# Gated linear attention followed by a GELU feed-forward: query scaling on GpSimd, with other group sizes and another load order

## The chip, the cores and the metric

The kernel runs on one core of one Trainium2 chip. The metric is the device time of one execution in microseconds; the kernel before has a median of 206.8 us in three runs (206.2 to 206.98). The profiled execution spans 205.2 us. A core has five engines that run their own instruction streams and meet at semaphores: TensorE (PE, with its weight loads as PEld), VectorE (DVE), ScalarE (ACT), GpSimd (POOL) and SyncE (SP, which here only issues DMAs).

## What is computed

For each of 4 batches and 8 heads, with 768 time steps and head dimension 48, a 48x48 state is decayed by a sigmoid gate, updated with an outer product and read by the query. The result, as 3072 tokens of 384 numbers, goes through a feed-forward with exact GELU.

```python
f = 1 / (1 + exp(-f_logit))                        # [4, 8, 768, 48]
for t in range(768):
    state = f[:, :, t, :, None] * state + einsum('bhd,bhe->bhde', k[:, :, t], v[:, :, t])
    y[:, :, t] = einsum('bhd,bhde->bhe', q[:, :, t], state)
x = y.transpose(0, 2, 1, 3).reshape(3072, 384)
out = gelu(x @ w_in) @ w_out                       # w_in 384x2048, w_out 2048x384
```

## The kernel before

The 3072 tokens are 24 chunks of 128, six per batch. Inside a chunk the recurrence is written with the running sum G of log f: keys are multiplied by exp(-G), queries by exp(G), and a masked 128x128 product per head takes the place of the loop. Across chunks a state is carried.

The Python program builds a list of operations, each with an engine, an assumed duration, its inputs and the buffers that it uses. A list scheduler (`Plan`) places them at assumed times, and the instructions are then emitted in the order of those times, so that each engine's stream is a fixed order worked out beforehand. An operation with `alt` may be placed on a second engine, if that lets it start earlier.

```python
for eng, dur in ((o.eng, o.dur),) if not o.alt else ((o.eng, o.dur), o.alt):
    ...                                    # t: when buffers, inputs and this engine are free
    cand.append((t, o, eng, dur))
for t, o, eng, dur in cand:
    ...
    key = (int((t + (self.bias if o.alt and eng == "ACT" else 0)) * 20 + 0.999), o.prio, o.seq, t + dur)
```

So the earliest start in steps of 0.05 us is taken, then the lowest priority number. The plan counts an input load as 1.05 us and gives weight DMAs a length on the DMA engines; it has no time on GpSimd for issuing one.

The settings, the weight load and the steps of a chunk n that matter here:

```python
SIZES = [4, 2, 2, 4, 4, 4, 4]              # chunks per feed-forward group
ORDER = ['c0', 'c1', 'c2', 'c3', 'O3', 'W0', 'W1', 'O1', 'c4', 'O0', 'O2']   # load order, then c5, c6, ...
EARLY = 1.5                                # weight DMAs are emitted this much ahead of their planned time
RMAJOR = 0; KBALT = 1; ALTN = 6; BIAS = 0.8; SEED = 0
BATCH = [1, 1, 1, 1, 1, 1, 2, 2, 2, 2, 2, 4, 2, 1, 1]    # chunks per exp/ln batch of the gate

def load_win(kk, half, ch):                # W0, W1: halves of the 2048 columns, 6 DMAs each
    p0, p1, r0 = ((0, 96, 96 * kk), (96, 128, 288 + 32 * kk))[half]
    cs = slice(ch * d_ff // 2, (ch + 1) * d_ff // 2)
    return nc.gpsimd.dma_start(out=win[p0:p1, kk, cs], in_=moe_w_in[r0:r0 + p1 - p0, cs])

# [...] chunk_in: f_logit, k, q, v of a chunk by four DMAs from SP
# [...] stage1: ACT exp, ACT ln -> lf; PE sums it into gps; ACT exp(G) -> gt, ACT exp(-G) -> rg
P.add("DVE", 0.57, ... nc.vector.tensor_tensor(kp, kt, rg, ALU.mult), name=f"KP{n}")     # L359
P.add("DVE", 0.57, ... nc.vector.tensor_tensor(qp, qt, gt, ALU.mult), name=f"QP{n}")     # L363
P.add("POOL", 0.52, ... nc.gpsimd.tensor_copy(vp, vt), name=f"VC{n}")                    # L369
# [...] attn: PE transposes kp and qp (L406); DVE copies kb, in two halves, for n < 6 on ACT if
#       earlier; ACT copies qT, for n < 6 on DVE if earlier; PE multiplies them (L425);
#       DVE masks the product into am (L429)
# state: PE S (L441), DVE R: rr = S + old (L456), POOL T: tn = rr * gl (L458), POOL SB: sb = bf16(tn), twice (L464)
# y: PE multiplies vp by am and sb by qT into yp (L477, L481)
# x: yp goes to xT by one copy (96x384) and three small ones (32x128), DVE, for n < 6 on ACT if earlier
# ffn_group: F1, PE: 3 matmuls win by xT per 512 columns of hps (L515); ACT gelu to gT (L519);
#            F2, PE: 16 matmuls gT by wout per chunk (L532); copy osb (L219 or L221); store by SP (L540)
```

A later pass makes the first load of a chunk wait for an earlier weight DMA, where weights were planned within 3 us before it: it takes the last weight DMA that was planned over 2.5 us before the load. Before the chain of work begins to fill the PE, short matmuls on a constant (`trin`, L587) are put into its gaps in the first 26 us.

Of the kernel before, what the change touches and what calls it, by code (L numbers as in the profile page):

```python
# [55 lines left out]
SWITCH = 1.28  # L56
JITTER = 2.0


class Op:  # L60
    __slots__ = ("eng", "dur", "fn", "bufs", "prio", "deps", "table", "start", "end", "vis", "seq", "name", "alt", "nb")


class Plan:


    def __init__(self, seed=0, bias=0.0):
        self.ops, self.w, self.r = [], {}, {}
        self.rnd, self.bias = random.Random(seed) if seed else None, bias

    def add(self, eng, dur, fn, rd=(), wr=(), bufs=(), prio=0.0, deps=(), table=None, name="", alt=None):
        o = Op()
        o.alt, o.nb = alt, 0.0
        o.eng, o.dur, o.fn, o.bufs, o.prio, o.table, o.name = eng, dur, fn, tuple(bufs), prio, table, name
        o.start = o.end = o.vis = None
        o.seq = len(self.ops)
        d = list(deps)
        for k in rd:
            d += self.w.get(k, [])
        for k in wr:  # L80
            d += self.w.get(k, []) + self.r.get(k, [])
        for k in rd:
            self.r.setdefault(k, []).append(o)
        for k in wr:
            self.w[k] = [o]
            self.r[k] = []
        o.deps = list({id(x): x for x in d if x is not o}.values())
        for b in o.bufs:
            b.users.append(o)
        self.ops.append(o)  # L90
        return o
# [7 lines left out]
    def run(self):  # L99
        free = {e: 0.0 for e in LAT}  # L100
        if self.rnd:
            for o in self.ops:
                o.prio += self.rnd.uniform(-JITTER, JITTER)
        act = None
# [7 lines left out]
        while left:  # L112
            best, stay, cand = None, None, []
            for o in left:
                ok = True
                t0 = o.nb
                for b in o.bufs:
                    v = b.ready()
                    if v is None:
                        ok = False  # L120
                        break
                    t0 = max(t0, v)
                if not ok:
                    continue
                for eng, dur in ((o.eng, o.dur),) if not o.alt else ((o.eng, o.dur), o.alt):
                    t = max(t0, free[eng])
                    for d in o.deps:
                        v = d.end if d.eng == eng and eng != "DMA" else d.vis
                        t = v if v > t else t
                    if o.table and o.table == act and (stay is None or t < stay):  # L130
                        stay = t
                    cand.append((t, o, eng, dur))
            for t, o, eng, dur in cand:
                if o.table and act and o.table != act and stay is not None and stay < t + 2 * SWITCH:
                    continue
                key = (int((t + (self.bias if o.alt and eng == "ACT" else 0)) * 20 + 0.999), o.prio, o.seq, t + dur)
                if best is None or key < best[0]:
                    best = (key, t, o, eng, dur)
# [25 lines left out]
def kernel(  # L164
# [10 lines left out]
    nc = tc.nc  # L175
# [11 lines left out]
    SIZES = [4, 2, 2, 4, 4, 4, 4]  # L187
    ORDER = ['c0', 'c1', 'c2', 'c3', 'O3', 'W0', 'W1', 'O1', 'c4', 'O0', 'O2']
    EARLY = 1.5
    WARM, FILL = 26.0, 0.75  # L190
    RMAJOR = 0
    LOCK = 12
    KBALT = 1
    ALTN = 6
    BIAS = 0.8
    SEED = 0
    CRING = 1
    HPB, ASB = 3, 3
    BATCH = [1, 1, 1, 1, 1, 1, 2, 2, 2, 2, 2, 4, 2, 1, 1]
    NG = len(SIZES)  # L200
# [13 lines left out]

    P = Plan(SEED, BIAS)

# [75 lines left out]
    def load_win(kk, half, ch):  # L292
        p0, p1, r0 = ((0, 96, 96 * kk), (96, 128, 288 + 32 * kk))[half]
        cs = slice(ch * d_ff // 2, (ch + 1) * d_ff // 2)
        return nc.gpsimd.dma_start(out=win[p0:p1, kk, cs], in_=moe_w_in[r0:r0 + p1 - p0, cs])
# [33 lines left out]
    def stage1(g):  # L329
# [13 lines left out]
        for n in ns:  # L343
# [18 lines left out]
                bufs=[x["kp"], x["kt"], rg], prio=pr, name=f"KP{n}")  # L362
            P.add("DVE", 0.57, lambda x=x, gt=gt: nc.vector.tensor_tensor(  # L363
                x["qp"].t()[:, :, 0:D], x["qt"].t(), gt.t(), ALU.mult),
                rd=[("gt", n), ("qt", n)] + [f"qpz{i}" for i in range(NQ)], wr=[("qp", n)],
                bufs=[x["qp"], x["qt"], gt], prio=pr + 1, name=f"QP{n}")

# [25 lines left out]
    def attn(n):  # L393
# [17 lines left out]
        for hh in range(2):  # L411
            P.add("DVE", 0.42, lambda hh=hh: copy(
                kb.t()[64 * hh:64 * hh + D, :, hh, :], tps[0].t()[64 * hh:64 * hh + D]),
                rd=[("tk", n), "kbz0", "kbz1"], wr=[("kb", n, hh)], bufs=[tps[0], kb], prio=pr + 4, name=f"KB{n}", alt=("ACT", 0.6) if KBALT and n < ALTN else None)
        P.add("ACT", 0.6, lambda: copy(qT.t(), tps[1].t()),
              rd=[("tq", n)], wr=[("qT", n)], bufs=[tps[1], qT], prio=pr + 4, name=f"QT{n}", alt=("DVE", 0.42) if n < ALTN else None)
        ams = []
# [70 lines left out]
        def cols():  # L488
            return slice(j * C, (j + 1) * C)
        P.add("DVE", 0.55, lambda: copy(xT.t()[0:96, :, cols()], yp.t()[0:96, 0:3 * C].rearrange("p (a t) -> p a t", t=C)),  # L490
              rd=[("yp", n, 0), ("yp", n, 1)], wr=[("x", n, 3)], bufs=[yp, xT], prio=pr + 2, name=f"X{n}", alt=("ACT", 0.51) if n < ALTN else None)
        for kk in range(KO):
            P.add("DVE", 0.29, lambda kk=kk: copy(
                xT.t()[96:128, kk, cols()], yp.t()[32 * kk:32 * kk + 32, 3 * C:4 * C]),
                rd=[("yp", n, 1)], wr=[("x", n, kk)], bufs=[yp, xT], prio=pr + 2, name=f"x{n}", alt=("ACT", 0.3) if n < ALTN else None)

    def ffn_group(g):
# [10 lines left out]
        for u in range(FO // pk):  # L508
            hps = r_hp.new()

            def f1(u=u, hps=hps):
                for i in range(pk):
                    fo = u * pk + i
                    for kk in range(KO):
                        nc.tensor.matmul(hps.t()[:, i * tok:(i + 1) * tok], win[:, kk, fo * 128:(fo + 1) * 128],  # L515
                                         xT.t()[:, kk, 0:tok], start=(kk == 0), stop=(kk == KO - 1))
            P.add("PE", 0.645 + 0.0025 * (3 * pk - 3), f1, rd=[("x", n, i) for n in ns for i in range(4)] + [f"win{u * pk // 8}"],
                  wr=[("h", g, u)], bufs=[xT, hps], prio=pr, deps=t["lockpe"], name=f"F1.{g}.{u}")
# [6 lines left out]
        for s_, r in ([(s_, r) for r in range(4) for s_ in range(s)] if g < RMAJOR  # L525
# [10 lines left out]
            if r < 3:  # L536
                continue
            P.add("ACT", 0.49, lambda op=op, osb=osb: copy(osb.t(), op.t()[:, 0:d_model]),
                  rd=[("o", n)], wr=[("os", n)], bufs=[op, osb], prio=pr - 1000, name=f"O{n}", alt=("DVE", 0.55) if n < ALTN else None)
            P.add("DMA", 0.6, lambda n=n, osb=osb: nc.sync.dma_start(out=out[n * C:(n + 1) * C, :], in_=osb.t()),  # L540
# [3 lines left out]
    for i, what in enumerate(order):  # L544
        if what[0] == "c":
            chunk_in(int(what[1:]), i)
        elif what[0] == "W":
            ch = int(what[1])
            P.w[f"win{ch}"] = [P.add("DMA", (1.2, 0.4)[half], lambda kk=kk, half=half, ch=ch: load_win(kk, half, ch),
                                     wr=[("win", kk, half, ch)], prio=i, name=f"win{ch}{kk}{half}")  # L550
# [94 lines left out]
```

## Time and profile before

| view | value |
|---|---|
| median of 3 runs | 206.8 us |
| span of the profiled execution | 205.2 us |
| PE busy | 188.4 us (92%), 14.0 us of it the short matmuls on a constant |
| DVE busy | 124.2 us (60%) |
| ACT busy | 135.7 us (66%) |
| POOL busy | 54.5 us (27%) |
| DMA engines | nine tenths or more busy nearly throughout the first 128 us, little after |

Shares of the whole span hide the stages. The kernel first waits for data, then has PE work in a row, and the DMA engines finish their loads at about 130 us. A row of the windows view gives for a stretch of time how long each engine was busy in it (with the number of its instructions), the clock granted to the PE, and the share and rate of the DMA engines; the stretch's length less the PE's busy time is time in which the PE stood still. The chain of waits goes back from the last instruction to what released it each time; in order of time it names what set the pace at each moment. GpSimd's DMA-issuing instructions carry a duration in the trace, but aren't counted as waits.

### The profile page before, as it was taken

To read this page: it belongs to the slowest core of one execution; us is meant where nothing else is said; L and a number is where in the kernel's file an instruction comes from. 1 tells how busy PE (TensorE), PEld (TensorE's weight loads), DVE (VectorE), ACT (ScalarE), POOL (GpSimd) and SP (SyncE) were. 2 spreads that over 40 slices of the span, in tenths; PEclk is the share of its full clock that TensorE was granted. 3 is DMA by queue.
4 is the path that set the end of the run, shared out by engine and by line. 5 is a ranking of instruction groups with operands and counts; after the bars stand their busy time and mean duration, and the time that the engine had idled before them with its cause. 6 is when DMAs were issued, how large, how long until landed. Compare 5 with 4: busy or idle time off the path is not lost.

```text
span 205.2 us, 4574 instructions
## 1 busy us (share of the span) xinstructions
PE 188.4 (92%) x1735; PEld 127.7 (62%) x1746; DVE 124.2 (60%) x270; ACT 135.7 (66%) x247; POOL 54.5 (27%) x117
## 2 busy tenths in 40 slices
PE   6798769988889987997999999999999999999993
PEld 5797734556568666865665668655676655644551
DVE  6598750019793899999999579964189862000000
ACT  4445349954588677986977973887977773169510
POOL 7238990004023134422344032030032200000000
PEclk9799999999999999999999999999999999999999
DMA  7999999999999999998999999300121000220022
GB/s 125 189 171 161 183 168 159 191 181 239 205 206 186 188 227 192 167 203 192 202 189 175 190 202 221 86 0 2 42 77 38 3 0 0 80 77 0 0 77 77
DMA packets 106388, 27.02 MB, mean 132 GB/s; under 512 B 100480, under 2 KB 105600, under 8 KB 106368
## 3 DMA queue, kind: packets, MB, share of 16 engines
q1 hardware_dynamic: 103296, 23.60, 64.4%
q0 software_dynamic: 3072, 3.15, 10.1%
q8 instruction: 13, 0.21, 0.5%
q14 instruction: 7, 0.06, 0.1%
HBM read 25.17 MB, written 4.72 MB: 146 GB/s over the span
## 4 chain that ended last, share of the span: by engine, by line
PE 66%; DVE 10%; SPq 8%; DMA 7%; issue 4%; ACT 2%; POOL 1%; DVEq 0%; ACTq 0%; POOLq 0%
PE hps L532 26%; PE hps L515 24%; SPq L326 7%; PE aps L477 4%; DMA fl<-in_f_logit_dram 4%; PE tp L406 4%; PE aps L425 3%; DVE am L429 3%; DVE xT L221 2%; DMA vt<-in_v_dram 2%; PE aps L481 2%; PE aps L441 1%; DVE qp L363 1%; DMA out_dram<-osb 1%; DVE kp L359 1%
## 5 line engine op out<-in xcount | busy, mean ns | idle before, releaser
L515 PE MATMUL hps<-xT,win 128*128 128x512 bf16 (+1 forms) x325 | 68.0, 347 | 2.8 <-DVE xT L221 2.1
L532 PE MATMUL hps<-wout,gT 128*128 128x384 bf16 x384 | 68.2, 326 | 0.0
L519 ACT ACTIVATE gT<-hps 128x512 bf16<-128x512 f32 x96 | 56.4, 597 | 12.5 <-PE hps L515 8.3
L532 PEld LDWEIGHTS <-gT 128*128 128x128 bf16 x384 | 36.4, 98 | 21.9
L515 PEld LDWEIGHTS <-win 128*128 128x128 bf16 x336 | 31.5, 98 | 26.3 <-issue 3.5
L221 DVE CAST xT<-aps 96x384 bf16<-96x384 f32 (+1 forms) x92 | 32.7, 355 | 9.2 <-PE aps L481 6.0
L429 DVE TENSOR_TENSOR am<-aps,mask 128x512 bf16<-128x512 f32 x48 | 31.0, 685 | 6.8 <-PE aps L425 6.4
L369 POOL CAST vp<-vt 128x384 bf16<-128x384 f32 x24 | 12.7, 530 | 62.7 <-DMA vt<-in_v_dram 37.3
L477 PE MATMUL aps<-am,vp 128*128 128x128 bf16 x192 | 19.9, 219 | 3.0 <-DVE am L429 2.6
L458 POOL TENSOR_TENSOR tn<-rr,gl 128x384 f32<-128x384 f32 x16 | 13.2, 827 | 30.5 <-DVE rr L456 21.9
L359 DVE TENSOR_TENSOR kp<-kt,rg 128x384 bf16<-128x384 f32 x24 | 14.6, 609 | 11.0 <-ACT rg L356 10.7
L219 ACT ACTIVATE osb<-hps 128x384 f32<-128x384 f32 x18 | 8.8, 490 | 18.6 <-PE hps L532 18.4
L477 PEld LDWEIGHTS <-vp 128*128 128x128 bf16 x192 | 15.5, 98 | 8.5 <-issue 3.5
L464 POOL CAST sb<-tn 48x192 bf16<-48x192 f32 x40 | 16.0, 399 | 12.3 <-PE aps L477 3.9
L221 DVE COPY kb<-tp 48x512 bf16<-48x512 bf16 x42 | 17.5, 418 | 0.6
L336 ACT ACTIVATE fl<-fl 128x384 f32<-128x384 f32 (+2 forms) x15 | 10.7, 714 | 10.5 <-DMA fl<-in_f_logit_dram 10.4
L356 ACT ACTIVATE rg<-aps 128x384 f32<-128x384 f32 x24 | 11.8, 491 | 7.2 <-PE aps L349 6.1
L604 ACT ACT_TABLE_LOAD x12 | 15.4, 1283 | 0.9 <-PEq L629 0.7
L587 PE MATMUL hps<-trin 128*128 128x128 bf16 x170 | 14.0, 242 | 1.4 <-POOL trin L231 1.4
L425 PE MATMUL aps<-qT,kb 128*128 128x128 bf16 x192 | 15.0, 221 | 0.3 <-DVE qT L221 0.3
L481 PE MATMUL aps<-qT,sb 128*128 128x128 bf16 x80 | 15.1, 219 | 0.0
L219 ACT ACTIVATE qT<-tp 128x512 bf16<-128x512 bf16 x18 | 10.7, 596 | 6.5 <-PE tp L406 6.4
(42 smaller groups left out, 174.0 us busy)
## 6 DMA issues: line engine op xcount, KB each, us to landing
fl<-in_f_logit_dram SPq DMA_DIRECT2D x24, 192.0 KB, 4.5
kt<-in_k_dram SPq DMA_DIRECT2D x24, 192.0 KB, 4.6
qt<-in_q_dram SPq DMA_DIRECT2D x24, 192.0 KB, 4.5
vt<-in_v_dram SPq DMA_DIRECT2D x24, 192.0 KB, 4.5
out_dram<-osb SPq DMA_DIRECT2D x24, 192.0 KB, 1.9
wout<-in_moe_w_out_dram POOLq DMA_DIRECT2D x4, 384.0 KB, 7.9
win<-in_moe_w_in_dram POOLq DMA_DIRECT2D x6, 192.0 KB, 4.8
win<-in_moe_w_in_dram POOLq DMA_DIRECT2D x6, 64.0 KB, 4.3
```

Source lines behind the costliest of these rows:

```text
L219: nc.scalar.activation(dst, src, AF.Copy)
L221: nc.vector.tensor_copy(dst, src)
L359: P.add("DVE", 0.57, lambda x=x, rg=rg: nc.vector.tensor_tensor(x["kp"].t()[:, :, 0:D], x["kt"].t(), rg.t(), ALU.mult), rd=[("rg", n), ("k ...
L425: nc.tensor.matmul(ap_.t()[:, i * C:(i + 1) * C], kb.t()[:, p, hh, :], qT.t()[:, p, :], start=True, stop=True)
L429: P.add("DVE", 0.69, lambda ap_=ap_, am=am: nc.vector.tensor_tensor(am.t(), ap_.t().rearrange("p (h t) -> p h t", t=C), mask.unsqueeze(1). ...
L464: nc.gpsimd.tensor_copy(sb.t()[64 * hh:64 * hh + D, :, D * hh:D * hh + D], tn.t()[64 * hh:64 * hh + D, :, D * hh:D * hh + D])
L477: nc.tensor.matmul(yp.t()[:, p * C:(p + 1) * C], vwin(vp.t(), 2 * p + hh), ams[half].t()[:, 2 * (p % 2) + hh, :], start=(hh == 0), stop=(h ...
L481: nc.tensor.matmul(yp.t()[:, p * C:(p + 1) * C], osb.t()[:, p, :], qT.t()[:, p, :], start=False, stop=True)
L515: nc.tensor.matmul(hps.t()[:, i * tok:(i + 1) * tok], win[:, kk, fo * 128:(fo + 1) * 128], xT.t()[:, kk, 0:tok], start=(kk == 0), stop=(kk ...
L519: acts.append(P.add("ACT", 0.6, lambda u=u, hps=hps: nc.scalar.activation(view()[:, u * pk:(u + 1) * pk, :].rearrange("p a b -> p (a b)"), ...
L532: nc.tensor.matmul(op.t()[:, 0:d_model], view()[:, fo, s_ * C:(s_ + 1) * C], wout[:, fo, :], start=(fo == 0), stop=(fo == FO - 1))
L604: nc.scalar.preload_act_table_set("natural_log_exp_and_others" if table == "exp" else "gelu_and_others")
```

## The change

Query scaling may go to GpSimd for every chunk, at an assumed 0.9 us there against 0.57 us on VectorE. The scheduler's random jitter is taken out, and a table of priorities by kind of operation comes in. With it come other settings: `w_in` is loaded in four quarters of its columns instead of two halves, the first of them ahead of chunk 3; gate batches have other sizes; the first feed-forward group may take its second product in the order of the weight's rows; the small copies may be placed on either engine in all 24 chunks without the 0.8 us handicap for ScalarE, and the `kb` copies on VectorE alone. The aim is to take work from VectorE and to have the feed-forward begin on part of `w_in`.

```diff
 SIZES = [4, 2, 2, 4, 4, 4, 4]
-ORDER = ['c0', 'c1', 'c2', 'c3', 'O3', 'W0', 'W1', 'O1', 'c4', 'O0', 'O2']
+ORDER = ['c0', 'c1', 'c2', 'W0', 'c3', 'W1', 'W2', 'W3', 'O0', 'O1', 'O2', 'c4', 'O3']
+NW = 4
-RMAJOR = 0
+RMAJOR = 1
-KBALT = 1
-ALTN = 6
-BIAS = 0.8
-SEED = 0
+KBALT = 0
+ALTN = 24
+BIAS = 0
+PRI = {'KP': 20, 'Y': -1, 'GE': 2, 'VC': 2, 'SB': 10, 'S': -10, 'GT': 1, 'Tq': 10, 'QT': -10, 'QP': -2, 'A': -10, 'Tk': -10, 'F': 2}
+QALTN = 24
-BATCH = [1, 1, 1, 1, 1, 1, 2, 2, 2, 2, 2, 4, 2, 1, 1]
+BATCH = [1, 1, 1, 1, 1, 2, 1, 2, 1, 2, 1, 2, 4, 1, 2, 1]
...
+def eng():
+    return nc.vector if P.cur.eng == "DVE" else nc.gpsimd
...
-cs = slice(ch * d_ff // 2, (ch + 1) * d_ff // 2)
+cs = slice(ch * d_ff // NW, (ch + 1) * d_ff // NW)
...
-P.add("DVE", 0.57, lambda x=x, gt=gt: nc.vector.tensor_tensor(
+P.add("DVE", 0.57, lambda x=x, gt=gt: eng().tensor_tensor(
     x["qp"].t()[:, :, 0:D], x["qt"].t(), gt.t(), ALU.mult),
     ...
-    bufs=[x["qp"], x["qt"], gt], prio=pr + 1, name=f"QP{n}")
+    bufs=[x["qp"], x["qt"], gt], prio=pr + 1, name=f"QP{n}",
+      alt=(("POOL", 0.9),) if n < QALTN else None)
...
-key = (int((t + (self.bias if o.alt and eng == "ACT" else 0)) * 20 + 0.999), o.prio, o.seq, t + dur)
+key = (int((t + (self.bias if eng != o.home else 0)) * 20 + 0.999), o.prio, o.seq, t + dur)
```

The group sizes of the feed-forward, the depths of the buffers and every formula stay as they are. What is left out above is the same rewriting of `alt` for the copies, the priorities added to each operation, and the first product's wait for its own quarter of `w_in`.

## Prediction, made before the changed kernel was run

> **What bounds the kernel now.** I began with the page's busy times.
>
> ```profile
> PE 188.4 (92%) x1735; PEld 127.7 (62%) x1746; DVE 124.2 (60%) x270; ACT 135.7 (66%) x247; POOL 54.5 (27%) x117
> ```
>
> The PE looks full, but its busy time holds fillers and tails, so I worked out how much it must do. The chain of waits in order of time shows runs of matmuls at full pace (start, length, what, how many):
>
> ```profile
> 61.58 3.27 PE hps L515 x30
> 66.16 0.45 PE aps L425 x8
> 104.43 0.65 PE hps L515 x3
> 170.71 10.40 PE hps L532 x64
> ```
>
> The second product costs 10.40/64 = 0.1625 us a matmul, times 384 is 62.4 us. The first costs 0.65 us per three 512-wide matmuls, with 80 such units in the five groups of four chunks: 52.0 us; the two groups of two have 96 narrower ones at 3.27/30 = 0.109: 10.5 us. A chunk's attention has 8 transposes, 8 products, 8 to 12 output matmuls (all at 0.45 per 8), and small ones: about 2.0 us, times 24 is 48. Sum 173 us. The PE's last matmul ends at 201.95 us by the chain, so 29 us of the PE are lost somewhere. The busy table by stage says where:
>
> ```profile
> core 0: us, PE busy (x) PEld busy (x) DVE busy (x) ACT busy (x) POOL busy (x), PEclk, DMA share, GB/s
> 16.00:29.00 13.00, 9.27 (x154) 8.63 (x155) 10.48 (x22) 5.37 (x13) 12.48 (x22) 1.00 1.08 171
> 45.00:58.00 13.00, 10.46 (x110) 6.96 (x108) 10.53 (x23) 7.62 (x18) 3.17 (x6) 1.00 1.08 216
> 72.00:98.00 26.00, 22.92 (x271) 17.61 (x268) 24.88 (x55) 21.15 (x42) 8.45 (x17) 1.00 1.13 197
> 98.00:130.00 32.00, 31.84 (x311) 21.55 (x312) 27.53 (x61) 24.51 (x41) 9.62 (x19) 1.00 1.17 193
> 130.00:202.00 72.00, 71.55 (x524) 42.64 (x527) 28.62 (x64) 45.82 (x85) 7.98 (x15) 1.00 0.09 33
> ```
>
> From 98 us to the end the PE stands still for 0.16 + 0.45 us: nothing that relieves another engine there can shorten the kernel. After 29 us the PE is lost for 13.00 - 10.46 = 2.5 us in the stage of group 1 (45 to 58) and for 26.00 - 22.92 = 3.1 us in that of groups 2 and 3 (72 to 98). In the latter VectorE is busy for 24.88 of 26 us, so it is VectorE's stage. All else, 21 us, is lost before the feed-forward's first matmul at 29.02 us. The chain around that start:
>
> ```profile
> 15.78 3.98 DMA vt<-in_v_dram
> ...
> 19.98 0.53 POOL win L295
> ...
> 20.51 0.36 POOL sb L464
> ...
> 20.91 0.65 POOL sb L464
> ...
> 21.62 0.72 POOL vp L369
> ...
> 29.02 1.02 PE hps L515 x4
> ```
>
> Chunk 3 has landed at 19.98, but its cast vp waits 1.6 us on GpSimd behind a weight issue and two state copies; then attention takes 7.4 us. GpSimd, 27% busy over all, is busy for 12.48 of 13 us here: the start is GpSimd's stage. The costs on it and the two scalings on VectorE, from the tiles' and lines' answers (min/median/max ns):
>
> ```profile
> L359 DVE TENSOR_TENSOR kp<-kt,rg x24: 548/559/946, 5.9 to 162.4; 128x384 bf16<-128x384 f32 x24
> L363 DVE TENSOR_TENSOR qp<-qt,gt x24: 549/553/766, 6.4 to 162.9; 128x384 bf16<-128x384 f32 x24
> L458 POOL TENSOR_TENSOR tn<-rr,gl x16: 822/827/840, 13.5 to 159.1; 128x384 f32<-128x384 f32 x16
> L295 POOL DMA_DIRECT2D win<-in_moe_w_in_dram x12: 497/510/560, 18.1 to 27.8; - x12
> ```
>
> **What the Trainium skill says.** "GPSIMD Engine Reference", section "Elementwise — side-by-side cycle accounting", gives about 2.6 cycles an element for a two-input operation on GpSimd at 1.2 GHz. For 384 elements that is an estimate of 0.83 us, and the trace's two-input operation of this size has 0.827. "SBUF — State Buffer", section "Who interferes with whom": a VectorE instruction with two SBUF inputs and a GpSimd instruction that reads SBUF exclude each other. The trace agrees as far as it goes: kp has a median of 559 ns and a longest of 946, and the longest begins at 76.44 next to a GpSimd cast at 77.04; the mask product, with one input from PSUM, holds its 685 ns. "DMA: Bandwidth & Descriptors", section "SWDGE vs HWDGE vs iDMA", has the descriptors of a GpSimd DMA made by GpSimd itself; here each w_in issue holds it for 510 ns, whether 192 or 64 KB. The same page, "Issuing engines are not separate DMA queues", says that all issuers share the same DMA engines: other orders move arrivals about but make no bandwidth. The trace shows a DMA share of 1.0 or more (overlapping packets) all through the loading.
>
> **The change part by part.**
>
> Query scaling. It goes to GpSimd where GpSimd can start it sooner; with kp sent to the back by its priority of 20 and VectorE crowded, I take 16 to 24 of the 24. Per scaling VectorE is rid of 0.59 us (mean 593 ns) and GpSimd gets 0.83. In the stage from 72 to 98 six scalings stand on VectorE, with 0.56, 0.69, 0.77, 0.55, 0.55 and 0.55 us: 3.7 us. VectorE falls from 24.9 to about 21.2 of 26 us, GpSimd rises from 8.5 to about 13.5. Of the 3.1 us lost there I count 2.0 as won: part of the waits is the length of the chain itself, and a scaling takes 0.27 us longer on GpSimd and has to take turns with kp.
>
> Copies free in all chunks. The page's xT group has 92 copies on VectorE, 32.7 us. Some can go to ScalarE, but ScalarE is at 21.15 of 26 us in that stage. At chunk 3's start the four copies of one chunk run one after another although on two engines (27.80, 28.39, 28.69). I count 0.3 us won.
>
> w_in in quarters, the first ahead of chunk 3. There are 24 issues instead of 12: 12 x 0.51 = 6.1 us more on GpSimd, nearly all between 12 and 35 us, and up to four scalings, 3.3 us, in the same stretch. The weights took the DMA engines some 20.8 us (their queue's 71.8% of the 29 us from 16 to 45 us), so a quarter of w_in, an eighth of the weights, is 2.6 us. Chunk 3 then lands near 22.6 instead of 20.0. Behind it stand the next quarters' issues: I let its cast come 2 to 2.5 us after its landing (now 1.6), and the first product near 32 instead of 29.
>
> That is not 3 us on the end. Group 1 begins at 57.66 now, and what holds it is chunk 5: the cast that needs its v is at 48.13, and 9.5 us later x is ready. The PE, starting at 32, needs 10.4 + 10.4 us for group 0 and some 4 for two chunks' attention, and would be done at about 57. So 29 to 32 is mostly taken from the slack before 57.66. What counts is chunk 5's arrival. The bytes ahead of it are the same, but chunk 4's first load is gated on O1 instead of the last piece of W1; GpSimd gets to O1 near 32.5 us, so it lands about 38, against a gate at 32.1 now. The DMA engines have O2 and O3 to move meanwhile, so I count 0.7 us later for group 1, plus 0.3 for a PE that has less slack.
>
> Row order in group 0, gate batches: group 0's second product follows its first without a gap now (39.38), so rows in order win nothing. Batches change when ScalarE's exp runs, over a PE that is full after 98. Zero each.
>
> Sum: -2.0 - 0.3 + 0.7 + 0.3 = -1.3 us, from 206.8 to 205.5.
>
> **The rivals.**
>
> First: GpSimd becomes the bound of the start. For it speak 12.48 of 13 us and the 6.1 + 3.3 us that come on top, in a plan that has no time for issues. If all of the 3 us and two more reach chunk 5's chain, group 1 begins at 62 and VectorE's relief gives 2 back: 206.8 + 4 - 2 = about 209. Against it: the loads still come one chunk per some 4.2 us, and the DMA engines have enough queued.
>
> Second: VectorE was the whole trouble after 58 us and more PE loss goes with it: all 3.1 us of its stage and 1 of the 2.5 in group 1, whose last steps are VectorE's copies and masks. Then 206.8 - 4 = about 202.8. For it speaks the 24.88 of 26 us; against it that group 1 waits on arrival.
>
> Third: the scalings on GpSimd block kp on VectorE and delay casts, and nothing is won: GpSimd's chain of a chunk (cast 0.5, scaling 0.83, tn 0.83, two sb 0.8) is 3 us of a pace of 5 to 7, so it fits on the average, but a scaling behind two sb copies is a microsecond late. That makes about 207.5.
>
> **Range and chances.** The middle is 205.5. The second rival gives 202.8 and the first 209; 8 in 10 should lie from 202.4 to 209.0. Over 2% faster is below 202.7, which takes nearly every lost microsecond after 29 us or an earlier start than I see: 0.13. Over 2% slower is above 210.9, which takes a start later by more than the first rival has: 0.09. Within 2%: 0.78.
>
> **What would show it right or wrong.** Right: qp is mostly a GpSimd operation near 0.83 us, longer beside kp; VectorE's busy time is down by 10 to 14 us and GpSimd's up by 15 to 20; 24 w_in issues near 0.5 us, GpSimd close to full from 16 to 34; the first L515 near 32 and group 1's near 58.5; a loss on the PE of 1 us or so between 72 and 98, and a PE without gaps from 98 on. Wrong: a first L515 at 29 or earlier; issues much shorter than 0.5 us for a quarter; a group 1 after 61 or before 56; qp mostly still on VectorE; or new gaps of the PE after 98 us, where I count on none.

## The result and the profile after

The changed kernel takes 213.87 us (median of 4 runs, 213.48 to 217.2), the kernel before 206.73 beside it: a ratio of 1.034, 95% interval 1.031 to 1.038. It is 7.1 us slower; the prediction had 1.3 us less, and its range ended at 209.0. The page's busy times:

```profile
PE 191.2 (90%) x1735; PEld 128.0 (60%) x1735; DVE 106.4 (50%) x220; ACT 143.0 (68%) x279; POOL 79.6 (38%) x150
```

VectorE lost 17.8 us of work, more than was expected, and GpSimd gained 25.1. What the change set out to do was done. The table by stage, for the stages that were shown of before (columns as there):

```profile
core 0: us, PE busy (x) PEld busy (x) DVE busy (x) ACT busy (x) POOL busy (x), PEclk, DMA share, GB/s
16.00:29.00 13.00, 8.73 (x132) 8.06 (x130) 7.86 (x18) 4.70 (x13) 12.39 (x25) 0.92 0.86 136
45.00:58.00 13.00, 11.82 (x106) 7.55 (x104) 5.49 (x12) 8.17 (x19) 4.90 (x8) 1.00 1.12 208
72.00:98.00 26.00, 23.22 (x258) 17.95 (x257) 19.83 (x40) 23.11 (x46) 12.49 (x19) 1.00 1.04 197
98.00:130.00 32.00, 30.17 (x284) 19.72 (x284) 18.82 (x42) 25.20 (x49) 12.34 (x22) 1.00 1.08 187
130.00:202.00 72.00, 71.53 (x547) 42.34 (x545) 31.63 (x65) 48.43 (x94) 15.48 (x24) 1.00 0.14 39
```

Three rows carry the story. From 16 to 29 us GpSimd is as full as before, but the DMA engines, at 1.08 and 171 GB/s before, are down to 0.86 and 136: as the experiments on the issues will show, they wait for something to move. The PE's granted clock is 0.92 there and was 1.00. From 72 to 98 VectorE has fallen from 24.88 to 19.83 us of 26, and the PE stands still for 2.78 us instead of 3.08: 0.3 won, where 2.0 were counted on. From 98 us to 202 it stands still for 1.83 + 0.47 us, where before it was 0.61; 1.3 us of this lie before group 3 begins at 100.75. Part of the chain of waits between 18 and 48 us, in order of time (start, length, what):

```profile
18.67 0.07 issue
18.74 0.32 POOL tn L459
...
21.23 0.99 POOL win L295 x3
...
22.66 1.48 POOL win L295 x3
...
24.20 0.99 POOL qp L363
25.19 0.99 POOL win L295 x2
26.18 0.51 POOL vp L370
26.69 1.10 POOL win L295 x3
...
31.66 0.44 POOL win L295
32.11 0.77 POOL wout L299
32.87 6.13 DMA wout<-in_moe_w_out_dram
...
39.05 0.37 SPq L322
...
42.86 4.98 DMA vt<-in_v_dram
```

This is GpSimd's list of work, one weight issue after another with casts and scalings between. At its end stands the last weight issue, behind that the load of chunk 4 (39.05, before 32.10), and behind that every later chunk. The operations in question:

```profile
L359 DVE TENSOR_TENSOR kp<-kt,rg x24: 546/559/1352, 6.1 to 163.0; 128x384 bf16<-128x384 f32 x24
L363 POOL TENSOR_TENSOR qp<-qt,gt x21: 982/997/1306, 7.6 to 162.6; 128x384 bf16<-128x384 f32 x21
L363 DVE TENSOR_TENSOR qp<-qt,gt x3: 551/552/553, 63.6 to 124.3; 128x384 bf16<-128x384 f32 x3
L295 POOL DMA_DIRECT2D win<-in_moe_w_in_dram x24: 495/505/724, 11.5 to 31.6; - x24
```

A quarter's issue holds GpSimd as long as a half's did: 505 ns for 96 or 32 KB, 510 for 192 or 64.

### The profile page after: what moved, and what is told of

It reads as the page before. It is cut to its first block, busy times and chain, and to the rows that moved or that the text cites. A ratio compares the mean times of both kernels' runs of the same rounds, so it can differ in the third digit from the quotient of the medians.

```text
span 211.6 us, 4538 instructions
## 1 busy us (share of the span) xinstructions
PE 191.2 (90%) x1735; PEld 128.0 (60%) x1735; DVE 106.4 (50%) x220; ACT 143.0 (68%) x279; POOL 79.6 (38%) x150
## 4 chain that ended last, share of the span: by engine, by line
PE 47%; DMA 13%; SPq 10%; POOL 9%; DVE 8%; ACT 6%; issue 4%; DVEq 0%; POOLq 0%; ACTq 0%
PE hps L533 19%; PE hps L516 18%; SPq L326 8%; DMA vt<-in_v_dram 6%; POOL win L295 4%; DMA wout<-in_moe_w_out_dram 3%; ACT xT L219 3%; PE aps L478 3%; DVE xT L221 2%; PE tp L407 2%; PE aps L426 2%; DMA fl<-in_f_logit_dram 2%; SPq L322 2%; POOL qp L363 2%; DVE am L430 2%
## 5 line engine op out<-in xcount | busy, mean ns | idle before, releaser
L516 PE MATMUL hps<-xT,win 128*128 128x512 bf16 (+1 forms) x336 | 68.8, 348 | 2.1 <-DVE xT L221 1.5
L520 ACT ACTIVATE gT<-hps 128x512 bf16<-128x512 f32 x96 | 54.9, 597 | 5.5 <-PE hps L516 2.7
L516 PEld LDWEIGHTS <-win 128*128 128x128 bf16 x336 | 31.4, 98 | 27.1 <-issue 2.4
L359 DVE TENSOR_TENSOR kp<-kt,rg 128x384 bf16<-128x384 f32 x24 | 18.0, 760 | 31.2 <-ACT rg L356 30.9
L363 POOL TENSOR_TENSOR qp<-qt,gt 128x384 bf16<-128x384 f32 x21 | 21.5, 1023 | 28.0 <-ACT gt L352 22.7
L219 ACT ACTIVATE xT<-aps 32x128 bf16<-32x128 f32 (+1 forms) x42 | 14.2, 339 | 26.1 <-PE aps L482 13.5
L221 DVE CAST xT<-aps 32x128 bf16<-32x128 f32 (+1 forms) x54 | 18.1, 335 | 19.0 <-ACT xT L219 13.2
L219 ACT ACTIVATE osb<-hps 128x384 f32<-128x384 f32 x18 | 8.8, 491 | 17.8 <-PE hps L533 17.7
L221 DVE COPY kb<-tp 48x512 bf16<-48x512 bf16 x48 | 20.1, 418 | 1.4 <-PE tp L407 0.5
L465 POOL CAST sb<-tn 48x192 bf16<-48x192 f32 x40 | 14.4, 361 | 12.7 <-DVE tn L453 4.4
L426 PE MATMUL aps<-qT,kb 128*128 128x128 bf16 x192 | 16.0, 223 | 1.8 <-ACT qT L219 0.7
L426 PEld LDWEIGHTS <-kb 128*128 128x128 bf16 x192 | 12.9, 100 | 4.1 <-DVE kb L221 0.8
```

The costliest lines, as they stand in the source:

```text
L219: nc.scalar.activation(dst, src, AF.Copy)
L221: nc.vector.tensor_copy(dst, src)
L359: P.add("DVE", 0.57, lambda x=x, rg=rg: nc.vector.tensor_tensor(x["kp"].t()[:, :, 0:D], x["kt"].t(), rg.t(), ALU.mult), rd=[("rg", n), ("k ...
L363: P.add("DVE", 0.57, lambda x=x, gt=gt: eng().tensor_tensor(x["qp"].t()[:, :, 0:D], x["qt"].t(), gt.t(), ALU.mult), rd=[("gt", n), ("qt", ...
L426: nc.tensor.matmul(ap_.t()[:, i * C:(i + 1) * C], kb.t()[:, p, hh, :], qT.t()[:, p, :], start=True, stop=True)
L520: acts.append(P.add("ACT", 0.6, lambda u=u, hps=hps: nc.scalar.activation(view()[:, u * pk:(u + 1) * pk, :].rearrange("p a b -> p (a b)"), ...
```

## Experiments

Sixteen kernels. Unless a text says otherwise the instruction order of every engine is that of the kernel it starts from. For the kernel of each experiment the text gives the median, the range of its runs, and its ratio to the kernel before (206.5 to 206.7 us beside them) with the 95% interval. "Last weight issue" and landings are read from the start of the last `wout` DMA and the landing times of the chunks' `v` loads in the trace; a group's start is its first L515 product (or that line's counterpart) after the group before has ended.

### The issues

**Fewer issues in the changed kernel.** Quarter 0 stays six DMAs; quarters 1 to 3 come in one set of six.

```diff
+        if ch > 1:
+            return None
+        cs = slice(0, d_ff // NW) if ch == 0 else slice(d_ff // NW, d_ff)
```

> The changed kernel, every stream in the same order, but quarters 1 to 3 of w_in are loaded by six DMAs in the place of eighteen (12 w_in issues instead of 24). Theory A (GpSimd's weight issues, which the plan has no time for, let the DMA engines run dry, so that the loads of chunk 4 and after it, and the feed-forward, come 5 us late): GpSimd is free of the issues some 6 us earlier, chunk 4's first load is issued near 33 instead of 39 us, group 1's first product comes near 58 instead of 62.1, and the time falls by 3.5 to 5 us from the changed kernel's 213.9, to 209 or 210. Rival R1 (the scalings themselves on GpSimd, which exclude kp on VectorE): the time stays within 1 us. Rival R2 (copies of one chunk spread over two engines): stays within 1 us.

210.5 us (210.12 to 211.92), 1.021 (1.015 to 1.026). The last weight issue moves from 34.34 to 29.71, group 1 from 62.08 to 58.14. Some 3 us of the 7.1 come back and no more.

**Twice as many in the kernel before.** Each of its 12 `w_in` DMAs is cut into two of half the columns, at the same place.

```diff
+        for h in range(2):
+            lo = ch * d_ff // 2 + h * d_ff // 4
+            cs = slice(lo, lo + d_ff // 4)
             r = nc.gpsimd.dma_start(...)
```

> The kernel before, in its own order, with each w_in DMA cut into two of half the columns at the same place: 24 issues instead of 12, nothing else. Theory A: the additional 6 us on GpSimd come in a stretch where it is full, so the gate on the last piece of W1 opens some 4 to 6 us later than 32 us, and the time rises by 3 to 5 us from 206.5, to 210 or 211. If the number of issues is not the cause (but the place of the quarters in the load order, or the scalings): within 1 us of the kernel before.

211.68 us (210.44 to 212.06), 1.024 (1.019 to 1.028): the doubled issues make this kernel 5.2 us slower. Its row of the stage table from 16 to 29 us:

```profile
16.00:29.00 13.00, 10.06 (x148) 9.71 (x146) 9.09 (x20) 4.78 (x11) 12.63 (x24) 0.87 0.99 152
```

Same bytes in smaller pieces, GpSimd full, DMA engines at 152 instead of 171 GB/s. The first product is only 1.2 us later (30.18), but chunks 5 and 11 both land 3.4 us later, group 1 begins at 61.08 and group 3 at 101.34. The DMAs are also half as large, which the next kernel leaves out.

**GpSimd's time without the DMAs.** Twelve memsets of a scratch tile, one after each of the 12 issues.

```diff
         r = nc.gpsimd.dma_start(...)
+        nc.gpsimd.memset(scratch, 0.0)          # 128x488 bf16
```

> The kernel before with its 12 weight issues as they are, and after each of them a memset of a 128x488 scratch tile on GpSimd, some 0.5 us, which nothing reads: GpSimd's time of 24 issues without the 12 further DMAs. If the issues cost by the time they hold GpSimd, this costs what 24 issues did: 210.8 to 212.3, chunks from the fifth on landing some 3.5 us later. If it was the number of DMAs or their smaller pieces, 206.2 to 207.0.

209.37 us (208.41 to 209.75), 1.012 (1.009 to 1.015): 2.7 us, between the two expectations.

```profile
L297 POOL MEMSET scratch<- x12: 504/523/531, 16.9 to 31.3; 128x488 bf16 x12
```

```profile
16.00:29.00 13.00, 9.92 (x140) 9.36 (x139) 8.90 (x19) 4.00 (x10) 12.53 (x27) 0.87 0.91 140
```

The memsets move no byte, and the DMA engines run short all the same. They delay the last weight issue by 3.46 us only (33.25 against 29.79; twice the issues, 4.99): part of them fell into time in which GpSimd was waiting. Per microsecond of that delay they cost 0.8 us, the doubled issues 1.0. So time on GpSimd is enough to cause the loss; that the smaller DMAs add a little is not excluded.

**Fewer in the kernel before.** The three row blocks of a half go in one DMA for each set of partitions: 4 issues instead of 12.

```diff
+        if kk == 0:
+            wmerged[half, ch] = nc.gpsimd.dma_start(out=win[p0:p1, :, cs],
+                in_=moe_w_in[r0:r0 + 3 * (p1 - p0), cs].rearrange("(a p) c -> p a c", a=3))
+        return wmerged[half, ch]
```

> The kernel before, every stream in its old order, with w_in in 4 DMAs instead of 12: the three blocks of a half in one DMA each for the 96 and for the 32 partitions, the same bytes to the same places. If an issue holds GpSimd for about 0.5 us whatever it moves, 4 us of it come free at the start and, at the 5.2 us that 12 further issues cost, up to 3 us of the time: 203.3 to 205.5, first L515 at 27 to 28. If the issue grows with the bytes (1.5 us each), or if the start is held by the loads themselves, 205.7 to 207.

204.97 us (204.54 to 206.45), 0.994 (0.991 to 0.996): faster than both kernels, by 1.7 us over the one before.

```profile
L298 POOL DMA_DIRECT2D win<-in_moe_w_in_dram x4: 603/646/693, 18.1 to 24.9; - x4
```

```profile
16.00:29.00 13.00, 9.85 (x156) 8.99 (x157) 10.99 (x23) 5.70 (x13) 10.21 (x16) 1.00 1.10 180
```

Three times the bytes hold GpSimd for 0.65 us instead of 0.51, GpSimd is busy for 10.2 of 13 us, and the DMA engines move 180 GB/s. The first product hardly moves (28.69); chunk 5 lands 2.8 us and group 1 begins 1.9 us sooner. Two thirds of the bytes also stand in the queue sooner, since they go with the first block; the run doesn't part this from GpSimd's free time.

**Two DMAs a quarter in the changed kernel**, by the same edit: 8 issues instead of 24.

> The changed kernel in its own order, w_in still in quarters of its columns, but each quarter in 2 DMAs instead of 6: 8 issues instead of 24. With quarters 1 to 3 in one set of six (12 issues in all) it took 210.5. If the number of issues is what counts: 208.5 to 210.5, chunk 11 landing at 77 or earlier. If the quarters as such cost (each product waiting for its own), it stays at 212 or more.

Its four runs, 209.02, 211.62, 212.4 and 212.97 us, lie too far apart to decide between the two expectations; the ratio, 1.018 (1.012 to 1.024), is that of the two undisturbed ones, the first two, and means about 210.4 us, no better than 12 issues gave.

**The gate of chunk 4's load taken out** of the changed kernel (`elif o.name in gates and o.name != "ldf4"`), to ask whether the wait for `wout` in the chain is the cause.

> The changed kernel in the same order, but chunk 4's first load doesn't wait for the landing of O1, the weight tile. Theory A, with the gate as the link between late issues and late chunks: the gap of the DMA engines between 18 and 37 us is filled by chunk 4, group 1's first product comes near 58, time 209 to 210.5. If the late issues act by the weights' own arrival instead: the time stays, or rises, as chunk 4 takes bandwidth from w_in. R1 and R2: within 1 us.

213.62 us (212.7 to 214.75), 1.034 (1.027 to 1.041): nothing. Chunk 4's load starts at 17.70 instead of 39.05, but in front of the weights. The DMA engines now move 186 GB/s from 16 to 29 us and 97 from 29 to 37, the last weight issue is at 35.66, and the first product goes from 31.77 to 33.08. Chunk 5 lands at 48.9, which is 2.9 us sooner than in the changed kernel, and group 1 begins at 62.89 all the same. From 33.08 on, the PE has 27.1 us of work before it, in 29.8 us. So a late first product holds group 1 as well as late chunks do: ScalarE takes up the gate of chunks 5 and 6 at 53.29, behind the copies of group 0's results, though its data are there at 49.94. Taking one of the two away wins nothing.

### The scalings

**On GpSimd in the kernel before**, all 24 (`nc.gpsimd.tensor_tensor` in L363).

> The kernel before, in its own order, with every query scaling on GpSimd at the place in the order where VectorE had it; loads and settings as before. R1 (the scalings are harmful by themselves): slower by 3 us or more. Theory A with the scalings as a smaller part: four scalings of 1.0 us in GpSimd's full stretch make the start some 2 us later, and VectorE's stage from 72 to 98 us gives back 1 to 2 us: between 206 and 209.

208.39 us (208.08 to 208.59), 1.010 (1.007 to 1.012): 1.9 us slower, VectorE's busy time between 72 and 98 us down to 22.74. Group 1 is 1.65 us late, and group 3 only 0.6.

**Only those of chunks 6 to 23.**

```diff
+ ... (nc.gpsimd if n > 5 else nc.vector).tensor_tensor(
```

> The kernel before, every stream in its old order, with the query scalings of chunks 6 to 23 on GpSimd and those of chunks 0 to 5 left on VectorE. Moving all 24 cost 1.9 us, and group 1 began 1.65 us later there. If the cost is only that GpSimd is full at the start, the start stays as before (first L515 near 29.0, group 1 near 57.7) and the time is 205.5 to 206.8. If the price is the turns that kp and qp have to take, or the longer scaling in a chunk's chain, it is paid in the later chunks too: 207.4 to 208.4.

206.71 us (205.54 to 208.9), 1.001 (0.999 to 1.004): no difference that shows.

```profile
72.00:98.00 26.00, 23.24 (x281) 18.47 (x281) 23.60 (x51) 21.95 (x44) 14.98 (x23) 1.00 1.14 201
```

So the cost was at the start, where GpSimd has no time to give. And the relief later is worth nothing that shows: VectorE is 1.3 us lighter in what I called its stage, the PE busier by 0.3, and group 3 begins at 97.07 instead of 97.34. Chunk 11 has landed at 76.2 (before 75.6).

**Back on VectorE in the changed kernel**, in its order (`if o.name.startswith("QP"): o.eng = "DVE"`).

> The changed kernel in the same order, with every query scaling on VectorE at the place in the order where GpSimd had it. R1: the pairs of kp and qp that took 2.6 us at 94 us go back to about 1.1 each, and the time falls by 4 us or more. Theory A, with the scalings as the second cause: the start stays near 31 us (a microsecond less on GpSimd there), the stall between 90 and 100 us loses 1 to 2 us, and the time falls by 1.5 to 3 us, to 211 or 212. If VectorE's relief was worth what I predicted (2 us), the time rises or stays.

215.5 us (215.2 to 217.89), 1.046 (1.039 to 1.053): slower still. The first product comes 2 us sooner (29.74), but group 3 0.8 us later (101.58). Neither R1 nor a fall of 1.5 to 3 us came true, but the rise that a relief of about 2 us would bring. In an order that was laid out with these operations off VectorE, moving them to GpSimd is worth 1.6 us (215.5 less 213.87), after what it costs at the start.

**Both loads on GpSimd in the kernel before**: 24 issues and 24 scalings, old order.

> The kernel before, old order, with both loads on GpSimd: 24 issues for w_in (each of the 12 cut in two at its old place) and all 24 scalings. Alone they cost 5.2 and 1.9 us. If both compete for the same GpSimd time at the start, they add up: 213.0 to 214.0, first L515 after 31, group 1 near 62.5, which is the changed kernel's time without any of its new order. If the second hides in the wait that the first makes (chunks arrive late anyway), 211.6 to 212.3, and some 2 us of the changed kernel's loss belong to its order.

213.27 us (213.17 to 213.36), 1.033 (1.030 to 1.036). They add up: 5.2 + 1.9 makes 7.1, measured 6.8. Group 1 comes at 64.51, 2 us later than expected.

```profile
16.00:29.00 13.00, 9.18 (x130) 8.52 (x128) 6.95 (x14) 4.67 (x11) 12.49 (x22) 0.87 0.88 132
```

The time is nearly that of the changed kernel, but not for the same reasons throughout: here the last weight issue is at 37.22, there at 34.34, because the changed order begins with a quarter of `w_in` at 11.55. What its order gained so, it gave back after group 3 (see the table).

### The order and the copies

**Every xT copy on VectorE** in the changed kernel (`if o.name[:1] in ("X", "x"): o.eng = "DVE"`), because the copies of one chunk hand over from engine to engine:

> The changed kernel in the same order, with all four copies of a chunk into xT on VectorE, as in the kernel before from chunk 6 on. R2 (copies that alternate between two engines wait for one another, and hold ScalarE's gelu and exp behind them): the 13.2 and 12.4 us of waits of VectorE and ScalarE for one another's xT copies are gone, the additional lateness after 115 us (2.8 us against the plan) goes, and the time falls by 2 to 3.5 us. If the copies on two engines are worth having, it rises by 1 us or more. Theory A alone: within 1 us.

216.3 us (215.59 to 217.05), 1.047 (1.042 to 1.053): worse by 2.4 instead of better by 2 to 3.5, so the trouble is not ScalarE as such.

**The copies of one chunk on one engine**, that of its large copy.

```diff
+    xeng = {o.name[1:]: o.eng for o in P.placed if o.name[:1] == "X"}
 ...
+        if o.name[:1] == "x": o.eng = xeng[o.name[1:]]
```

> The changed kernel in the same order, with the three small copies of a chunk into xT on the engine of its large one (15 chunks ScalarE, 9 VectorE), so that both engines keep about their load and no copy waits for the other engine. R2 in its second form (the hand-over between engines costs, the load doesn't): 1.5 to 3 us less than the changed kernel's 213.9. If all four on VectorE was slower because copies on two engines do overlap: 1 us or more slower.

212.83 us (212.61 to 213.64), 1.032 (1.029 to 1.035): 1.0 us less by the medians, but the interval overlaps that of the changed kernel (1.031 to 1.038), and 1.5 to 3 were expected. A gain is not shown. The timeline of the changed kernel shows why one was possible (start, length, engine, line; in brackets the idle time and what ended it):

```profile
166.35 0.55 DVE L221 CAST xT<-aps 96x384 bf16<-96x384 f32 x1 [0.33 <-PE aps L482]
...
166.94 0.26 ACT L219 ACTIVATE xT<-aps 32x128 bf16<-32x128 f32 x1 [0.33 <-DVE xT L221]
167.24 0.29 DVE L221 CAST xT<-aps 32x128 bf16<-32x128 f32 x1 [0.33 <-ACT xT L219]
167.56 0.27 ACT L219 ACTIVATE xT<-aps 32x128 bf16<-32x128 f32 x1 [0.35 <-DVE xT L221]
```

Four copies from parts of one PSUM tile into parts of one `xT` tile, on two engines, run one after another, each waiting for the one before. Which of the two tiles orders them, the trace doesn't say. A second engine doesn't shorten the four copies of a chunk.

**Fewer issues and copies on one engine together.**

> Six instead of eighteen DMAs for quarters 1 to 3 of w_in and the copies of a chunk on one engine together, in the changed kernel's order. If both causes stand and are separate: 210.5 less 1.5 to 3 us, 207.5 to 209. If the second cause is not one: 210.5 again.

210.23 us (209.33 to 211.01), 1.018 (1.015 to 1.022). With the last weight issue at 29.48 and chunk 11 landed at 75.9, group 3 begins at 95.22, 2.1 us ahead of the kernel before, and the end is 3.8 us behind it. The copies are worth nothing that shows beside few issues (210.5 without them).

```profile
98.00:130.00 32.00, 31.07 (x279) 20.26 (x280) 18.63 (x38) 26.08 (x48) 11.27 (x19) 0.98 1.06 177
130.00:211.00 81.00, 73.93 (x539) 43.66 (x545) 27.56 (x58) 47.35 (x93) 12.68 (x21) 0.99 0.11 36
```

Its PE is busy for 105.0 us after 98 us; the kernel before for 31.84 + 71.55 = 103.4. It is not that more attention is left: when group 3 begins, 88 transposes of `kp` and `qp` and 96 products with `vp` are still to come in both kernels, and in the changed one. The same work takes longer in this order, and where it does the table below shows.

**All three costs taken away**: 8 issues, copies on one engine, the scalings of chunks 0 to 5 on VectorE.

> The changed kernel with the three costs found so far taken away at once, order unchanged: quarters by 8 DMAs, the four xT copies of a chunk on one engine, the scalings of chunks 0 to 5 on VectorE. If these were all of the loss, it comes to 205.5 to 207.5, level with the kernel before or ahead of it. If the order that was planned on wrong durations costs by itself, as the 2 us left between this kernel with few issues and the kernel before with its scalings on GpSimd say, 207.8 to 210.

211.35 us (209.53 to 211.93), 1.021 (1.017 to 1.025): no better than the last, and above both expectations. Yet the start is mended: group 3 begins at 96.62, 0.7 us ahead of the kernel before. The whole loss, some 4 us, now lies behind that point, and is the order's.

**Two new orders from a plan that knows the measured costs.**

> The changed program with a plan that knows what was measured: each weight issue holds GpSimd (0.51 us for w_in, 0.78 for w_out), kp and an operation of GpSimd take turns, the four copies of a chunk run one after another, a scaling takes 1.0 us on GpSimd. Priorities, batches and load order were searched anew for the earliest planned end of the PE, with w_in in quarters and 16 chunks free to scale on GpSimd. Planned end of the PE 201.05 us, that of the kernel before 201.24 (201.95 in its trace, time 206.5). If what made the changed kernel lose was what its plan did not know, the chip follows this plan within 1.5 us: 205.5 to 207.5. If quarters starve the DMA engines in a way that this plan does not hold either, the first L515 comes 2 us or more behind it and the time is 209 to 212.

208.68 us (208.56 to 209.34), 1.011 (1.008 to 1.014): better than the changed kernel by 5, not level with the one before. This order puts only 7 scalings on GpSimd. The first product comes 1.3 us after the plan's (34.96 against 33.65), the start of the second product 3.4 us (48.88 against 45.48). Between them the PE had only part of its clock (0.84 in the next 8 us):

```profile
29.00:37.00 8.00, 4.48 (x41) 2.98 (x39) 3.75 (x8) 5.88 (x15) 5.00 (x10) 0.74 1.19 187
```

From there on it keeps about that distance (204.2 against 201.05 at the end).

> The same plan with the measured costs and searched settings, but w_in in halves by 12 DMAs and the load order of the kernel before, and only 8 chunks free to scale on GpSimd. Planned end of the PE 201.95 us. If the chip follows such a plan: 206.3 to 208.0. If the order as such costs time that no plan here knows (banks of PSUM held longer, copies that wait for each other), 209 or more even without the added issues.

215.28 us (215.17 to 216.87), 1.044 (1.040 to 1.049): its second product begins 8.9 us behind its plan (57.82 against 48.91), its last matmul ends 8.0 behind. Only 3 scalings are on GpSimd. The chain shows the cause:

```profile
28.92 4.95 DMA win<-in_moe_w_in_dram
33.87 0.02 SPq L326
33.89 0.05 issue
33.94 9.14 DMA fl<-in_f_logit_dram
```

A chunk's first load took 9.14 us to land behind queued weights, where the plan counts 1.05, and the PE was busy for 0.56 us of the 8 from 37 to 45. So counting the issues is not enough for a plan; the queue on the DMA engines has to be in it too, and my guess that the missing durations were all that was wrong fell for the start.

### All runs side by side

The last column but one is the time from the start of group 3 to that of group 6, the last. The kernel with two DMAs a quarter is left out.

| kernel | last weight issue | chunk 5 landed | group 1 | group 3 | group 3 to 6 | against before |
|---|---|---|---|---|---|---|
| before, 4 issues | 27.69 | 45.3 | 55.80 | 95.43 | 83.6 | -1.7 |
| before | 29.79 | 48.1 | 57.66 | 97.34 | 83.6 | |
| before, late scalings moved | 29.81 | 48.3 | 57.91 | 97.07 | 84.1 | +0.2 |
| before, all scalings moved | 30.69 | 48.7 | 59.31 | 97.97 | 84.1 | +1.9 |
| before, memsets | 33.25 | 49.8 | 59.44 | 99.75 | 83.6 | +2.7 |
| before, 24 issues | 34.78 | 51.5 | 61.08 | 101.34 | 83.6 | +5.2 |
| before, both | 37.22 | 53.9 | 64.51 | 103.18 | 84.1 | +6.8 |
| after, three costs away | 29.35 | 48.5 | 58.61 | 96.62 | 88.3 | +4.7 |
| after, fewer issues, copies | 29.48 | 47.3 | 57.60 | 95.22 | 88.8 | +3.8 |
| after, fewer issues | 29.71 | 47.1 | 58.14 | 97.85 | 87.9 | +4.0 |
| after, scalings on VectorE | 33.72 | 51.2 | 61.99 | 101.58 | 87.8 | +9.0 |
| after, copies on one engine | 34.34 | 52.0 | 61.57 | 99.60 | 87.0 | +6.4 |
| after | 34.34 | 51.8 | 62.08 | 100.75 | 86.6 | +7.1 |
| after, copies on VectorE | 34.98 | 52.5 | 62.50 | 101.63 | 89.2 | +9.8 |
| after, no gate | 35.66 | 48.9 | 62.89 | 101.80 | 86.4 | +7.2 |
| new order, quarters | 38.36 | 47.5 | 62.31 | 100.01 | 83.3 | +2.2 |
| new order, halves | 33.57 | 49.9 | 72.64 | 104.94 | 84.1 | +8.8 |

In the old order the time follows the last weight issue: (6.8 + 1.7) / (37.22 - 27.69) = 0.9 us for each microsecond. The changed order has a similar trend, some 4 us higher. Most of these 4 us are in the last column but one: every kernel in the old order needs 83.6 to 84.1 us from group 3 to group 6, every kernel in the changed order 86.4 us or more, whatever else was mended.

The PE's granted clock is a rival to all this. In the traces it falls to a half for 3.4 us or more, now here and now there; in the changed kernel just ahead of the first product,

```profile
27.00:30.40 3.40, 3.40 (x36) 3.40 (x34) 1.85 (x3) 0.00 (x0) 3.38 (x7) 0.50 0.76 93
```

and with fewer issues from 94.3 to 101.1 us. But several kernels have runs with the full clock throughout: 210.12 us with fewer issues, 209.33 with the copies besides, 210.44 with 24 issues in the old order, 208.41 with memsets, 204.7 with 4 issues (median of four), and 206.2 for the kernel before (median of twenty). So the clock is part of these differences, up to 1 us, and not their cause. The changed kernel itself has no such run.

## Why the prediction was wrong

**The facts of the change** came as predicted: `qp` on GpSimd in 21 of 24 chunks, 24 issues of 0.5 us, GpSimd full from 16 us on, the first product at 31.77 ("near 32"). That last hit is luck: chunk 3 landed at 21.6 and not 22.6, its cast came 4.6 us behind it and not 2 to 2.5, and attention then took 5.6 us instead of 7.4, in spite of the half clock. The scaling takes 1.0 us instead of the 0.83 that I took from `tn`, an operation of the same size with float output.

**The step that failed is the start**: "I count 0.7 us later for group 1, plus 0.3". Group 1 came at 62.08, 4.4 us later. I did see that chunk 5's arrival sets it, and that GpSimd would reach the `w_out` issues near 32.5 (32.11). But I said that "the DMA engines have enough queued". They had not (kernel before, changed kernel):

```profile
16.00:45.00 29.00, 25.20 (x239) 16.76 (x241) 11.33 (x24) 18.18 (x33) 14.54 (x25) 1.00 1.07 173
16.00:45.00 29.00, 23.60 (x213) 15.88 (x211) 8.64 (x20) 17.46 (x34) 18.46 (x35) 0.94 0.98 150
```

23 GB/s less for 29 us is 0.67 MB not moved, at the 197 GB/s of later stages 3.4 us. Chunk 5 landed 3.7 us later, chunk 11 5.2, the last one 6.3 (136.4 against 130.1). I took GpSimd's issues for a delay of the first product, "mostly taken from the slack". They are the supply of the DMA engines, and what these missed early was not made good: they stay full until the loads end. Nor was there that slack: I counted 10.4 + 10.4 + 4 = 24.8 us of PE work up to group 1, and the changed kernel has 27.3 busy us there (its order transposes chunk 6 first as well), so that it would be done at 59.1 without any wait. And the gate batches, which I had at zero, act here: chunk 5's gate is computed together with chunk 6's (first the kernel before, then the changed one):

```profile
44.97 0.52 ACT L336 ACTIVATE fl<-fl 128x384 f32<-128x384 f32 x1 [2.40 <-DMA fl<-in_f_logit_dram]
52.81 0.84 ACT L336 ACTIVATE fl<-fl 128x768 f32<-128x768 f32 x1 [0.45 <-DMA fl<-in_f_logit_dram]
```

Chunk 5's `f_logit` had landed at 48.6, chunk 6's at 52.78. In the nine kernels of the changed order group 1 begins 8.6 to 9.7 us after this batch, so it is tied to chunk 6's `f_logit` and not to chunk 5's. No run takes the batch apart, so its share of the 4.4 us isn't known. That the issues bound the start is the first rival; its group 1 at 62 was exact, and its "about 209" too low because it gave VectorE's relief back and left out the order. Fewer issues take about 3.1 us of the 7.1 away (7.1 - 4.0).

**"Of the 3.1 us lost there I count 2.0 as won"**: 0.3 in the changed kernel's row, nothing in the old order with the late scalings moved. By the groups' starts the changed kernel makes good 1.0 us between group 1 and group 3 (4.4 us late, then 3.4), with chunk 6's transposes already done. I called the stretch from 72 to 98 us VectorE's because VectorE was 24.88 of 26 us busy. Busy isn't bound: with 1.3 us less of VectorE's work there, nothing was won. Arrival may be the bound (in all the runs of the table group 3 begins 19.2 to 23.0 us after chunk 11 has landed), but that is argued: the spread is larger than what was to be won. That the move is worth about 1.6 us in the changed order shows only when it is taken back there. The third rival, turns with `kp`, is seen in the trace but costs little by itself: the late scalings pay it and lose nothing.

**"I count 0.3 us won"** for the copies: one engine for all four of a chunk is faster by 1.0 us, or by 0.3 with fewer issues, and neither is clear of the noise.

**"Zero each"** for row order and gate batches, over a PE that is full after 98: the batch of chunks 5 and 6 acts before that, and the order as a whole costs some 4 us (3.8 to 4.7 in the kernels with few issues), of which 3.0 us lie between group 3 and group 6 in the changed kernel (86.6 us against 83.6). Little of that is a gap that the rows show: from group 3 on the PE stands still for 1.0 us instead of 0.5. The program's own plan has 83.8 us for this stretch and the PE done at 197.9, that of the kernel before 83.9 and 201.2; in the traces the PE is done at 208.3 and 201.9. The two new orders, planned with the turns of `kp`, the copies one after another and the issues, take 83.3 and 84.1 us for it, where their plans have 83.5 and 85.0. So the changed order is one that its plan misjudged. Which of the missing durations misled it is open: neither the copies on one engine (87.0) nor the scalings back on VectorE (87.8) brings the old 83.6 back, and priorities, batches and row order were not tried one by one.

Two slips of the working change nothing: what is lost ahead of 29.02 us is 29 - 0.6 - 2.5 - 3.1 = 22.8 us, not 21, and the longest `kp`, at 76.44, runs beside `tn` (76.15 to 76.98) before it meets the cast at 77.04.

## What to carry over

An engine that issues the DMAs is part of the supply of data: count its issues in time, and see in the stage table what the DMA engines have moved by the end of the start, before giving it other work. One row is not enough: with all three costs away they move 139 GB/s from 16 to 29 us, but 187 in the next 8, and group 3 is early. The cheap gain was fewer, larger DMAs for the same bytes: 1.7 us, where moving 18 scalings won nothing. An order that is planned with assumed durations can be no better than these; compare the planned with the traced start of one late stage before trusting a shorter plan.

## What the runs showed of the hardware

The time for which an issue holds GpSimd hardly depends on the bytes: 0.51 us for 32 to 192 KB, 0.65 for 192 or 576 KB in three blocks, 0.78 for 384 KB of `w_out`. The Trainium skill ("DMA: Bandwidth & Descriptors", section "SWDGE vs HWDGE vs iDMA") says who makes the descriptors; that the cost goes far more by the issue than by the byte, these runs show.

When `kp` on VectorE meets `qp` on GpSimd, both take longer, as the same skill's "SBUF — State Buffer", section "Who interferes with whom", leads one to expect. Two of each in the changed kernel's timeline, in which two alone would take 2.0 and 1.1 us:

```profile
94.52 2.26 POOL L363 TENSOR_TENSOR qp<-qt,gt 128x384 bf16<-128x384 f32 x2
94.63 2.56 DVE L359 TENSOR_TENSOR kp<-kt,rg 128x384 bf16<-128x384 f32 x2
```

The mean of `kp` rises from 0.61 to 0.76 us over the kernel. VectorE's own relief by the 21 scalings, 21 x 0.59 = 12.4 us, is so reduced by 24 x 0.15 = 3.6; the rest of the 17.8 us that it lost are copies that went to ScalarE.
